# Attention in front of two feed-forward layers: scores as two 64-row products, the softmax reciprocal on GpSimd, evacuations re-dealt

## The chip, the core and the metric

One core of one Trainium2 chip runs the whole program. The metric is device time in microseconds of one execution; several executions of the kernel are timed and the median is compared. Engines are named as the profile names them: PE is TensorE, PEld its weight loads, DVE is VectorE, ACT is ScalarE, POOL is GpSimd, SP is SyncE, which issues nearly all the transfers of the stage that matters here.

## The reference

Windowed attention over 4 batches of 8 heads (576 positions, 64 elements a head; half of the heads see the last 32 positions, the other half every fourth of the last 128), then a gated layer, then a second layer, all in float32:

```python
    scores = scale * np.matmul(q, k.transpose(0, 1, 3, 2))
    ...
    scores = np.where(masks[None, :, :, :], scores, -1000000000.0)
    scores = scores - np.max(scores, axis=-1, keepdims=True)
    attn = np.exp(scores)
    attn = attn / (np.sum(attn, axis=-1, keepdims=True) + 1e-09)
    return np.matmul(attn, v).astype(np.float32)
...
    g = x @ w_gate
    silu = g * (1.0 / (1.0 + np.exp(-g)))
    val = x @ w_val
    return (silu * val @ w_out).astype(np.float32)
...
    h = x @ w_in
    g = h - np.tanh(h)
    return (g @ w_out).astype(np.float32)
```

The first layer is 512 to 1536 to 512, the second 512 to 2048 to 512, on 2304 tokens.

## The kernel before

**Attention.** The work is cut into 48 units. A unit is one pair of heads and three blocks of 64 queries; positions of the dilated heads are laid out so that every block needs 96 neighbouring keys. For each unit SP loads a tile `q` (L452; the queries of the two heads stand block-diagonally with zeros beside them, so that the tile's 128 rows are head 0's 64 elements and head 1's 64, and the keys behind them) and a tile `v` (L453). Then, in this order:

- `scores`, PE L419: three products of 128 rows by 128 columns, 96 keys wide, into one PSUM bank `ps`. A product in float32 leaves two records in the trace, so a unit has six.
- `maxima`, DVE L424: mask and row maximum. `exps`, ACT L430: exponentials and their row sums `sm`.
- `invert`, DVE L434 and L435: adds 1e-9 to `sm` (128 x 3) and takes the reciprocal.
- `norm`, POOL L438: multiplies the exponentials by it.
- `turn`, PE L444: three transpositions into a bank `pt`. `evac`: copies `pt` to SBUF, on DVE (L448) for every second unit and on ACT (L450) for the others.
- `mix`, PE L476, once for three units: products with `v`, 64 columns wide, the two heads in the two halves of the output; then ACT L489 and DVE L492 write them, split in two float32r parts, to the tiles `x` of the first layer.

**Layers.** Weights come by SP (L315) and are converted by ACT L318 and DVE L322, L326, L331, L300, L303. Each layer is made of products that PE runs in blocks: L508 (first tiles of layer 1, going up, six records a block), L519 (the seven-product scheme, going up and down), L775 and L795 (going down).

**Order.** A planner (`Plan.order`) simulates tasks with costs and priorities written as constants, and each engine's instructions are then emitted in the order of its start times. On the chip every engine runs its own list in that order and waits where a semaphore makes it. `Plan.fill` puts products on a constant tile (`idle`, L398) into PE's list where the planner saw PE idle. The constants that the change touches: `LEAD` and `SLACK` (how early a weight is loaded, how much later than its modelled landing it may be used), `DELAY_7` (how long a down product stands back), `SECOND` (spacing of the first group's weights), `FIRST_FAR` (assumed latency between engines).

Of the kernel before, what the change touches and what calls it, by code (L numbers as in the profile page):

```python
# [11 lines left out]
F32 = mybir.dt.float32  # L12
# [8 lines left out]
WINDOW, DIL = 32, 4  # L21
# [68 lines left out]
class Task:  # L90
    def __init__(self, n, eng, dur, prio, emit, deps, bufs, gives, lat, port, work):
        self.lat, self.n, self.eng, self.dur, self.prio, self.emit = lat, n, eng, dur, prio, emit
        self.port, self.work = port, work
        self.deps, self.bufs, self.gives = [d for d in deps if d is not None], list(bufs), gives
        self.fresh = None
        self.then, self.ready, self.start, self.left = [], 0.0, None, len(self.deps)


class Plan:
    ENGINES = ("PE", "DVE", "ACT", "POOL", "DMA", "NONE")  # L100

    def __init__(self, rings):
        self.tasks, self.free = [], {r: list(range(n)) for r, n in rings.items()}

    def add(self, eng, dur, prio, emit, deps=(), bufs=(), gives=None, lat=None, port=False, work=0.0):
# [6 lines left out]
    def rates(self, queues):  # L112
        heads = [e for e in queues if queues[e]]
        return [queues[e] for e in heads], [DMA_SHARE[e] for e in heads] if len(heads) > 1 else [1.0]

    def order(self):
        for t in self.tasks:
# [7 lines left out]
        while True:  # L125
            moved = True
            while moved:
                moved = False
                for e in self.ENGINES:
                    if busy[e] > now:  # L130
                        continue
                    best = None
                    for t in waiting[e]:
                        if t.ready > now + 1e-9 or (best is not None and (t.prio, t.n) >= (best.prio, best.n)):
                            continue
                        if t.port and port[0] != e and port[1] > now + 1e-9:
                            continue
                        need = {}
                        for b in t.bufs:
                            if b.slot is None:  # L140
                                need[b.ring] = need.get(b.ring, 0) + 1
                        if all(len(self.free[r]) >= n for r, n in need.items()):
# [7 lines left out]
                    best.start, busy[e] = now, now + best.dur  # L150
                    if best.port:
# [56 lines left out]


NEAR, FAR = 0.2, 0.7  # L210
FIRST_FAR, ATT_FAR = 0.3, 0.5
ISSUE, LAUNCH, LAND = 0.45, 1.1, 0.7
DMA_SHARE = {"DMA": 0.4, "POOL": 0.6}

ATT0, ATT_STEP = -30.0, 0.3
CONV0 = -24.0
LEAD = 28
DELAY = 7
ON_DVE = {(2, 1)}
SEEDED = {(1, 2), (1, 3)}  # L220
DELAY_7 = 8
MM = 0.174
V_LATE, MASK_LATE, PLAIN_FIRST = 10, 4.0, True
TOGETHER, FEW, SOON = 3, 2, 0
PASSING = 0
SECOND = 2.0
IDLE, SPARE, IDLE_UNTIL = 0.214, 0.5, 60.0
Y_SOON, DELAY_7D = 30.0, 11.0
APART = {(1, 0, 0), (1, 0, 1)}
SLACK = 2.0  # L230
SUM_DMA = 3.9
Q_DMA, V_DMA, W_DMA = 1.12, 0.5, 1.65
QUICK = 0.5
HURRY = 20.0
WARM = 10
# [8 lines left out]
def attention_then_two_ffns(ctx, tc, qk, vt, masks, w1, w2, out):  # L244
# [33 lines left out]
    new_q = ring("q", [P, UN * P + UT + WINDOW], F32)  # L278
# [7 lines left out]
    make_identity(nc, ident)  # L286
    alpha = const.tile([P, 1], F32, name="alpha")
    nc.gpsimd.memset(alpha, ALPHA)
    nthr = const.tile([P, 1], F32, name="nthr")
    nc.gpsimd.memset(nthr, -THR * THR)  # L290
    warm = const.tile([P, 512], mybir.dt.bfloat16, name="warm")
# [117 lines left out]
    def attention(b, hp, g, prio, evac_on):  # L409

        q, v, e, nm, sm, at = new_q(), new_v(), new_e(), new_nm(), new_sm(), new_at()
        ps, pt = new_ps(), new_ps()
        kinds = MASK_OF[hp // (NP // 2)][UN * g:UN * g + UN]
# [38 lines left out]
        a = add_att("DMA", ISSUE, prio, lambda: nc.sync.dma_start(out=q(), in_=qk[b, hp, g]), bufs=[q], lat=NEAR, work=Q_DMA)  # L452
        got_v = add_att("DMA", ISSUE, prio + V_LATE, lambda: nc.sync.dma_start(out=v(), in_=vt[b, hp, g]), bufs=[v], lat=NEAR, work=V_DMA)  # L453
# [7 lines left out]
        a.fresh = idle(pt)  # L461
        a = add_att(evac_on, 0.48 if evac_on == "DVE" else 0.38, prio, evac, [a], [pt, at])
        return (b, hp, g), v, at, [a, got_v]

# [78 lines left out]
            res.append((ps, a))  # L543
        return res

    def seven_up(c1, c2, sums, parts, prio):
# [18 lines left out]
        def sum22():  # L565
            nc.vector.tensor_tensor(out=e(), in0=pe()[:, :TT], in1=e(), op=ALU.add)

        p1 = pe_task(pa, (wa, 0), B11, True, [], [pb, pe])
        p5 = pe_task(pe, (w31, 1), T1, True, [], [pa, pb])
        soon = prio - HURRY  # L570
        sb = plan.add("ACT", 0.39, soon, lambda: seed(pb, pa), [p1], [pa, pb], lat=QUICK)
        ke = plan.add("ACT", 0.39, soon, keep, [p5], [pe, e], lat=QUICK)
        c11 = pe_task(pa, (wa, 1), B21, False, [sb])
        p6 = pe_task(pb, (w24, 0), T2, False, [sb])
        sc = plan.add("ACT", 0.39, soon, lambda: seed(pe, pb), [p6, ke], [pb, pe], lat=QUICK)
# [19 lines left out]
    def times_gate(g, a, prio, whole):  # L595
        s = new_t()

        def tanh():
            nc.scalar.activation(out=s(), in_=g()[:, :TT], func=AF.Tanh, scale=0.5)
# [5 lines left out]
            nc.scalar.activation(out=s(), in_=g()[:, :TT], func=AF.Silu)  # L605

        if whole:
            return s, plan.add("ACT", 0.39, prio, silu, [a], [g, s])
# [345 lines left out]
    def finish(layer, h, prio, raw=False):  # L954
        if layer == 1:
            (g, a), v = h
            whole = state["k"] >= 2
            return times_val(times_gate(g, a, prio, whole), v, prio, 1.0 if whole else 0.5, raw)
        (h, a), = h
        return cubic(h, a, prio)  # L960

# [6 lines left out]
    for layer, sizes in ((1, GROUPS1), (2, GROUPS2)):  # L968
        k = 0
        for turn, n in enumerate(sizes):  # L970
# [25 lines left out]
            for p in order:  # L996
# [3 lines left out]
                more = {"early": early} if layer == 2 and last else {}  # L1000
                if p in sevens:
                    blocks = parts_of(p, before == (layer, p), when - 12.0, begun)
                    q = [seven_up(ws[0][c], ws[1][c], extra[c], blocks, when + 0.01 * c) for c in ups]
# [191 lines left out]
```

## Time and profile before

| | before |
|---|---|
| median of 3 timed executions | 880.81 us (879.83 to 880.93) |
| the profiled execution, its own time | 881.28 us |
| its span, first to last instruction | 879.5 us |
| granted TensorE clock, mean | 0.998 |

The span is what the trace shows; 1.8 us of the profiled execution's time lie around it. Times in a trace count from the span's start. A record of PE is one matrix instruction; their ends are modelled, so starts tell more than ends.

### The profile page before, as it was taken

How to read it: one execution, taken by the hardware profiler on the slowest of the kernel's cores; microseconds unless marked ns; L12 is line 12 of the kernel's file. 1: busy time of each engine (PE TensorE's matmuls, PEld its weight loads, DVE VectorE, ACT ScalarE, POOL GpSimd, SP SyncE). 2: the span in 40 equal slices, each digit the busy share in tenths (PEclk: the TensorE clock that was granted, in tenths of full speed). 3: DMA queues.
4: the chain of work that ended last, by engine and by line, in shares of the span. 5: the costliest groups of instructions: out<-in, count | busy, mean ns of one | idle time of the engine just before them, and what ended most of it. 6: DMA issues, size and time to landing. Idle time of an engine off the chain costs nothing.

```text
span 879.5 us, 15336 instructions
## 1 busy us (share of the span) xinstructions
PE 864.4 (98%) x5240; PEld 814.5 (93%) x5242; DVE 729.1 (83%) x1738; ACT 584.2 (66%) x1516; POOL 88.3 (10%) x116
## 2 busy tenths in 40 slices
PE   8999999999999999999999999999999999999996
PEld 5789999999999999999999999889989989898995
DVE  6999999988788788788759999898787777765675
ACT  6889857768668668568658787666666656564540
POOL 2333300000000000000000000001101010111100
PEclk9999999999999999999999999999999999999999
DMA  9999353675785785777895558899979796968995
GB/s 276 282 281 266 111 205 131 228 247 173 195 258 122 208 246 122 208 225 195 252 322 215 207 199 320 255 202 270 218 220 225 177 253 165 229 131 207 248 295 213
DMA packets 48951, 193.53 MB, mean 220 GB/s; under 512 B 5600, under 2 KB 10720, under 8 KB 48864
## 3 DMA queue, kind: packets, MB, share of 16 engines
q1 hardware_dynamic: 40224, 145.28, 48.0%
q0 software_dynamic: 8640, 47.19, 29.1%
q8 instruction: 43, 0.70, 0.3%
q14 instruction: 44, 0.36, 0.1%
HBM read 119.31 MB, written 73.14 MB: 219 GB/s over the span
## 4 chain that ended last, share of the span: by engine, by line
PE 91%; DVE 4%; DMA 3%; ACT 1%; issue 0%; POOL 0%; SPq 0%; ACTq 0%; POOLq 0%
PE ps L519 53%; PE ps L795 23%; PE ps L775 7%; PE ps L508 3%; PE ps L419 2%; DMA q<-qk 2%; PE ps L476 2%; DMA st<-w 1%; PE ps L444 1%; DVE e L424 1%; PE ps L914 1%; DVE x L492 0%; ACT e L430 0%; DVE u L331 0%; DVE u L326 0%
## 5 line engine op out<-in xcount | busy, mean ns | idle before, releaser
L519 PE MATMUL ps<-x,wc 128*128 128x384 f32 x2316 | 427.2, 336 | 0.0
L519 PEld LDWEIGHTS ps<-x,wc 128*128 128x128 f32 x2316 | 407.3, 188 | 4.6
L795 PE MATMUL ps<-wc,y 128*128 128x512 f32 (+1 forms) x870 | 208.7, 391 | 0.0
L795 PEld LDWEIGHTS ps<-wc,y 128*128 128x128 f32 x870 | 161.9, 188 | 32.2 <-ACT acc L688 0.4
L688 ACT ACTIVATE acc<-ps 128x512 f32<-128x512 f32 (+1 forms) x134 | 74.7, 560 | 71.9 <-PE ps L795 56.8
L715 POOL DMA_DIRECT2D sum<-acc x60 | 52.6, 876 | 673.9 <-ACT acc L688 259.7
L590 DVE TENSOR_TENSOR y<-t,y 128x384 fp32r<-128x384 f32 x168 | 92.2, 553 | 26.4 <-ACT y L587 26.2
L587 ACT ACTIVATE y<-t 128x384 fp32r<-128x384 f32 x168 | 86.4, 518 | 23.7 <-DVE t L655 9.5
L530 ACT ACTIVATE ps<-ps 128x384 f32<-128x384 f32 x156 | 73.7, 476 | 24.1 <-PE ps L519 20.1
L300 ACT ACTIVATE wc<-u 128x512 fp32r<-128x512 f32 x108 | 67.3, 631 | 27.1 <-PE ps L519 19.9
L303 DVE TENSOR_TENSOR wc<-u,wc 128x512 fp32r<-128x512 f32 x108 | 74.3, 697 | 5.7 <-ACT wc L300 4.1
L563 DVE TENSOR_TENSOR ps<-ps,t 128x384 f32<-128x384 f32 x56 | 31.5, 562 | 41.0 <-PE ps L519 40.9
L775 PE MATMUL ps<-y,wc 128*128 128x384 f32 x336 | 62.9, 337 | 0.0
L652 DVE SCALAR_TENSOR_TENSOR t<-t 128x384 f32<-128x384 f32 x96 | 52.7, 550 | 8.8 <-ACT t L649 8.2
L775 PEld LDWEIGHTS ps<-y,wc 128*128 128x128 f32 x336 | 58.8, 188 | 0.1
L430 ACT ACTIVATE e<-e,nm 128x96 f32<-128x96 f32 x144 | 52.0, 368 | 8.0 <-DVE nm L424 8.0
L649 ACT ACTIVATE t<-ps 128x384 f32<-128x384 f32 x72 | 35.0, 486 | 28.9 <-DVE ps L563 17.8
L318 ACT ACTIVATE u<-st 128x512 f32<-128x512 f32 x68 | 44.9, 666 | 12.6 <-DMA st<-w 9.5
L326 DVE SCALAR_TENSOR_TENSOR u<-st,u 128x512 uint32<-128x512 uint32 x68 | 46.8, 691 | 0.6
L331 DVE SCALAR_TENSOR_TENSOR u<-st,u 128x512 uint32<-128x512 uint32 x68 | 46.7, 689 | 0.4
L519 PE MATMUL ps<-y,wc 128*128 128x384 f32 x198 | 45.3, 337 | 0.0
L419 PE MATMUL ps<-q 128*128 128x96 f32 x288 | 39.7, 278 | 5.2 <-DMA q<-qk 2.5
(87 smaller groups left out, 1095.2 us busy)
## 6 DMA issues: line engine op xcount, KB each, us to landing
x<-part SPq DMA_DIRECT2D x66, 768.0 KB, 7.1
sum<-acc POOLq DMA_DIRECT2D x60, 768.0 KB, 9.3
st<-w SPq DMA_DIRECT2D x68, 512.0 KB, 6.7
q<-qk SPq DMA_DIRECT2D x48, 304.0 KB, 7.3
sum<-acc SPq DMA_DIRECT2D x12, 768.0 KB, 5.6
part<-x SPq DMA_DIRECT2D x12, 768.0 KB, 3.9
acc<-sum SPq DMA_DIRECT2D x12, 768.0 KB, 7.3
v<-vt SPq DMA_DIRECT2D x48, 144.0 KB, 7.2
```

Of the source, the lines that this page charges most:

```text
L300: nc.scalar.activation(out=w()[:, 0, :], in_=u(), func=AF.Copy)
L303: nc.vector.tensor_tensor(out=w()[:, 1, :], in0=u(), in1=w()[:, 0, :].bitcast(F32), op=ALU.subtract)
L419: nc.tensor.matmul(ps()[:, i * KT:(i + 1) * KT], lhsT=q()[:, i * P:(i + 1) * P], rhs=q()[:, k0:k0 + KT], start=True, stop=True)
L519: nc.tensor.matmul(ps()[:, :TT], lhsT=w()[:, i, c:c + P], rhs=rhs, start=(start and n == 0), stop=(n == 3 * len(cols) - 1), skip_group_che ...
L530: nc.scalar.activation(out=ps()[:, :TT], in_=src()[:, :TT], func=AF.Copy)
L587: nc.scalar.activation(out=y()[:, 0, :], in_=s(), func=AF.Copy)
L590: nc.vector.tensor_tensor(out=y()[:, 1, :], in0=s(), in1=y()[:, 0, :].bitcast(F32), op=ALU.subtract)
L652: nc.vector.scalar_tensor_tensor(out=sq(), in0=sq(), scalar=E0 / E1, in1=sq(), op0=ALU.add, op1=ALU.mult)
L688: nc.scalar.activation(out=o, in_=ps()[:, :c1 - c0], func=AF.Copy)
L715: nc.gpsimd.dma_start(out=keep, in_=at(), accum_op=ALU.add)
L775: nc.tensor.matmul(ps()[:, :TT], lhsT=w[2][0]()[:, a, m * P:(m + 1) * P], rhs=y[0]()[:, bb, :], start=(start and n == 0), stop=(n == 3 * l ...
L795: nc.tensor.matmul(ps()[:, :c1 - c0], lhsT=y[0]()[:, a, s * P:(s + 1) * P], rhs=w[1][0]()[:, bb, c0:c1], start=(n == 0), stop=(n == 3 * le ...
```

## The change

Three edits in `attention`, and new constants and rules in the planner, which put every engine's list in another order.

- The product of two heads becomes two products, rows 0 to 63 into output partitions 0 to 63 and rows 64 to 127 into 64 to 127, each with 64 columns and 96 keys. The zeros of `q` are no longer read; the transfer that brings the tile is the same (`Q_PARTS = 1`).
- `invert` goes to POOL: an addition and a `pow` with exponent -1 (a constant tile `minus`), both 128 x 3.
- Evacuations are dealt DVE, DVE, ACT in turn.

```diff
-FIRST_FAR, ATT_FAR = 0.3, 0.5
+FIRST_FAR, ATT_FAR = 0.4, 0.5
...
-LEAD = 28
+LEAD = 25
...
-DELAY_7 = 8
+DELAY_7 = 6
 MM = 0.174
+SCORES = 0.56
+INVERT, INV_POOL = 'POOL', 0.5
+EVAC = ('DVE', 'DVE', 'ACT')
+LEAVE, KEEP_T = (5, 6), 1
...
-SECOND = 2.0
+SECOND = 1
...
-SLACK = 2.0
+SLACK = 1.5
...
+Q_PARTS, V_POOL, ISSUE_POOL = 1, False, 0.62
...
+                        if t.takes and (len(self.free["t"]) < (KEEP_T if t.takes == "t" else 0) or any(b.slot is None for c in self.older(t.case) for b in c[t.takes])
+                                        or t.takes == "ps" and any(b.slot is None for b in t.case["x"])):
+                            continue
+                        if t.leave and sum(b.slot is not None and b.users > 0 for b in self.fronts) >= t.leave:
+                            continue
...
             for i in range(UN):
-                k0 = UN * P + QT * i
-                nc.tensor.matmul(ps()[:, i * KT:(i + 1) * KT], lhsT=q()[:, i * P:(i + 1) * P],
-                                 rhs=q()[:, k0:k0 + KT], start=True, stop=True)
+                k0 = (UT if Q_PARTS == 3 else UN * P) + QT * i
+                for h2 in range(2):
+                    of, c = slice(D * h2, D * h2 + D), QT * i if Q_PARTS == 3 else P * i + QT * h2
+                    nc.tensor.matmul(ps()[of, i * KT:(i + 1) * KT], lhsT=q()[of, c:c + QT],
+                                     rhs=q()[of, k0:k0 + KT], start=True, stop=True)
...
         def invert():
-            nc.vector.tensor_scalar_add(sm(), sm(), 1e-9)
-            nc.vector.reciprocal(out=sm(), in_=sm())
+            if INVERT == "DVE":
+                nc.vector.tensor_scalar_add(sm(), sm(), 1e-9)
+                nc.vector.reciprocal(out=sm(), in_=sm())
+            else:
+                nc.gpsimd.tensor_scalar_add(sm(), sm(), 1e-9)
+                nc.gpsimd.tensor_tensor(out=sm(), in0=sm(), in1=minus, op=ALU.pow)
...
-        a = add_att("PE", 0.67, prio, scores, [a], [ps, q])
-        a.fresh = idle(ps)
+        a = add_att("PE", SCORES, prio, scores, got_q, [ps, q])
+        a.fresh, a.leave = idle(ps), LEAVE[0]
...
-        a = add_att("DVE", 0.31, prio, invert, [a], [sm])
+        a = add_att(INVERT, 0.31 if INVERT == "DVE" else INV_POOL, prio, invert, [a], [sm], port=INVERT == "POOL")
...
-        fronts.append(attention(*unit, ATT0 + ATT_STEP * n, ("DVE", "ACT")[n % 2]))
+        fronts.append(attention(*unit, ATT0 + ATT_STEP * n, EVAC[n % len(EVAC)]))
```

`LEAVE` lets the planner start a unit's scores only while fewer than five of the stage's banks are taken, and its transposition while fewer than six are. `KEEP_T` and `takes` hold the products and copies of a seven-product block that feeds another one back until the blocks begun before it have their buffers.

PE's list, from the 26th unit's scores to the block behind the 32nd's, before (`q` marks scores, `ident` a transposition, `at,v` a mix, `x,wc` a block of layer 1):

```order
L419 MATMUL ps_1009<-q_810 128x96 x3
L508 MATMUL ps_1026<-x_346,wc_884 128x384 x6
L444 MATMUL ps_1044<-ident,e_912 96x128 x3
...
L419 MATMUL ps_1095<-q_861 128x96 x3
L419 MATMUL ps_1111<-q_879 128x96 x3
L444 MATMUL ps_1125<-ident,e_940 96x128 x3
L508 MATMUL ps_1026<-x_448,wc_884 128x384 x6
...
L419 MATMUL ps_1224<-q_1006 128x96 x3
L444 MATMUL ps_1237<-ident,e_1090 96x128 x3
L419 MATMUL ps_1244<-q_1024 128x96 x3
L508 MATMUL ps_1257<-x_694,wc_356 128x384 x6
```

and with the change, over the same units:

```order
L440 MATMUL ps_1091<-q_843 64x96 x6
L547 MATMUL ps_1112<-x_380,wc_961 128x384 x6
L547 MATMUL ps_1131<-x_766,wc_375 128x384 x6
...
L440 MATMUL ps_1198<-q_928 64x96 x6
L547 MATMUL ps_1112<-x_483,wc_961 128x384 x6
L440 MATMUL ps_1237<-q_950 64x96 x6
L440 MATMUL ps_1249<-q_988 64x96 x6
L469 MATMUL ps_1262<-ident,e_1140 96x128 x3
L547 MATMUL ps_1131<-x_485,wc_375 128x384 x6
...
L440 MATMUL ps_1359<-q_1100 64x96 x6
L440 MATMUL ps_1370<-q_1110 64x96 x6
L547 MATMUL ps_1386<-x_766,wc_782 128x384 x6
```

Two more blocks of layer 1 stand between these scores: ahead of the 32nd unit's scores PE's list has ten of them instead of eight, with 26 transpositions and 8 mixes as before, and four more filler products.

SP's list up to the 32nd `q`, before:

```order
L452 DMA q_861<-qk 128x608
L315 DMA st_868<-w 128x512
L452 DMA q_879<-qk 128x608
L452 DMA q_910<-qk 128x608
L452 DMA q_927<-qk 128x608
L453 DMA v_979<-vt 96x384
L453 DMA v_990<-vt 96x384
L453 DMA v_997<-vt 96x384
L452 DMA q_1006<-qk 128x608
L452 DMA q_1024<-qk 128x608
```

and with the change:

```order
L487 DMA q_928<-qk 128x608
L333 DMA st_933<-w 128x512
L487 DMA q_950<-qk 128x608
L492 DMA v_965<-vt 96x384
L487 DMA q_988<-qk 128x608
L492 DMA v_1051<-vt 96x384
L492 DMA v_1062<-vt 96x384
L487 DMA q_1069<-qk 128x608
L492 DMA v_1083<-vt 96x384
L487 DMA q_1100<-qk 128x608
L487 DMA q_1110<-qk 128x608
```

Only the places of the `v` transfers move here: at the 32nd `q` both lists have issued 32 `q`, 26 `v`, 6 weights and the masks.

POOL's list gains two instructions for each unit, here of the third and fourth unit with the change:

```order
L459 TENSOR_SCALAR sm_187<-sm_187 128x3
L460 TENSOR_TENSOR sm_187<-sm_187,minus 128x3
L463 TENSOR_TENSOR e_143<-e_143,sm_170 128x288
L463 TENSOR_TENSOR e_165<-e_165,sm_187 128x288
L459 TENSOR_SCALAR sm_212<-sm_212 128x3
```

Before, POOL's list held the third kind alone; a unit's multiplication may now stand behind the next unit's reciprocal.

## Rows read from the trace of the kernel before

**Rows 1.** The page: span, and busy time, share and instructions of each engine.

```profile
span 879.5 us, 15336 instructions
PE 864.4 (98%) x5240; PEld 814.5 (93%) x5242; DVE 729.1 (83%) x1738; ACT 584.2 (66%) x1516; POOL 88.3 (10%) x116
```

**Rows 2.** Five stretches: length, busy per engine (records), PE clock, DMA share, GB/s.

```profile
0.00:20.00 20.00, 17.11 (x126) 11.82 (x128) 12.08 (x73) 12.48 (x52) 4.76 (x14) 1.00 0.91 277
20.00:66.30 46.30, 42.04 (x495) 37.58 (x495) 44.76 (x256) 40.70 (x200) 15.81 (x22) 1.00 1.04 282
66.30:112.60 46.30, 46.29 (x553) 43.55 (x553) 44.42 (x230) 39.44 (x188) 15.16 (x21) 1.00 0.63 176
112.60:860.00 747.40, 746.60 (x4011) 711.22 (x4010) 618.74 (x1166) 489.91 (x1076) 52.59 (x60) 1.00 0.77 218
860.00:879.50 19.50, 12.36 (x62) 10.36 (x60) 9.13 (x18) 1.63 (x4) 0.00 (x0) 0.91 0.55 202
```

**Rows 3.** The chain that ended last, 57 to 100: start, length, what.

```profile
57.30 8.87 DMA q<-qk
...
66.31 0.88 PE ps L419 x6
...
68.26 0.33 PE ps L444 x3
68.58 1.05 PE ps L508 x6
...
70.29 0.64 PE ps L419 x6
70.93 1.20 PE ps L476 x36
72.13 0.46 PE ps L444 x3
...
97.57 1.20 PE ps L476 x36
98.77 1.25 PE ps L508 x6
```

**Rows 4.** DMA issues, 0 to 110: count, KB each, median us to landing.

```profile
q<-qk SPq DMA_DIRECT2D x48, 304.0 KB, 7.3
v<-vt SPq DMA_DIRECT2D x48, 144.0 KB, 7.2
```

**Rows 5.** PE's waits in 20 to 66.3: in total, times, longest.

```profile
PE ps L419 <- DMA q<-qk: 1.1, 2, 0.7
PE ps L419 <- DVE nm L424: 1.1, 3, 0.5
```

**Rows 6.** Blocks L508 alone, by stretch: PE busy (records), PEld busy (records).

```profile
20.00:66.30 46.30, 10.38 (x48) 8.00 (x48) 1.00 1.04 282
66.30:112.60 46.30, 17.19 (x84) 14.19 (x84) 1.00 0.63 176
```

**Rows 7.** Groups by line, 0 to 110: count, busy, mean ns, idle before.

```profile
L438 POOL TENSOR_TENSOR e<-e,sm 128x288 f32<-128x288 f32 x48 | 35.0, 731 | 71.6 <-DVE sm L435 22.8 <-ACT e L430 16.0 <-PE ps L444 10.1
...
L448 DVE COPY at<-ps 96x384 f32<-96x384 f32 x23 | 12.5, 544 | 1.3 <-PE ps L444 1.3
...
L450 ACT ACTIVATE at<-ps 96x384 f32<-96x384 f32 x24 | 12.0, 498 | 5.0 <-PE ps L444 4.8
L434 DVE TENSOR_SCALAR sm<-sm 128x3 f32<-128x3 f32 x48 | 11.4, 237 | 0.9 <-ACT e L430 0.9
...
L435 DVE RECIPROCAL sm<-sm 128x3 f32<-128x3 f32 x48 | 8.4, 176 | 1.7
...
L288 POOL MEMSET alpha<- 128x1 f32 x1 | 0.1, 99 | 0.0
```

**Rows 8.** Waits after 100 that touch weights or PE: in total, times, longest.

```profile
ACT u L318 <- DMA st<-w: 9.5, 6, 3.5
...
PE ps L519 <- ACT ps L530: 0.8, 1, 0.8
```

More of the change, by code (lines that the diff above doesn't have):

```diff
@@ L94, in __init__ @@
         self.deps, self.bufs, self.gives = [d for d in deps if d is not None], list(bufs), gives
-        self.fresh = None
+        self.fresh, self.leave, self.case, self.takes = None, 0, None, False
         self.then, self.ready, self.start, self.left = [], 0.0, None, len(self.deps)
@@ L102, in __init__ @@
     def __init__(self, rings):
+        self.begun, self.fronts = [], []
         self.tasks, self.free = [], {r: list(range(n)) for r, n in rings.items()}
@@ L114, in rates, with older @@
         return [queues[e] for e in heads], [DMA_SHARE[e] for e in heads] if len(heads) > 1 else [1.0]
+    def older(self, case):
+        return self.begun[:next((i for i, c in enumerate(self.begun) if c is case), None)]
     def order(self):
@@ L141, in order @@
                                 need[b.ring] = need.get(b.ring, 0) + 1
-                        if all(len(self.free[r]) >= n for r, n in need.items()):
+                        if all(len(self.free[r]) >= n  for r, n in need.items()):
                             best = t
@@ L150, in order @@
                     best.start, busy[e] = now, now + best.dur
+                    if best.case is not None and not any(c is best.case for c in self.begun):
+                        self.begun.append(best.case)
                     if best.port:
@@ L288, in attention_then_two_ffns @@
     nc.gpsimd.memset(alpha, ALPHA)
+    minus = const.tile([P, UN], F32, name="minus")
+    nc.gpsimd.memset(minus, -1.0)
     nthr = const.tile([P, 1], F32, name="nthr")
@@ L412, in attention @@
         ps, pt = new_ps(), new_ps()
+        plan.fronts += [ps, pt]
         kinds = MASK_OF[hp // (NP // 2)][UN * g:UN * g + UN]
@@ L450, in evac @@
                 nc.scalar.activation(out=at(), in_=pt()[:KT, :UN * P], func=AF.Copy)
-        a = add_att("DMA", ISSUE, prio, lambda: nc.sync.dma_start(out=q(), in_=qk[b, hp, g]), bufs=[q], lat=NEAR, work=Q_DMA)
-        got_v = add_att("DMA", ISSUE, prio + V_LATE, lambda: nc.sync.dma_start(out=v(), in_=vt[b, hp, g]), bufs=[v], lat=NEAR, work=V_DMA)
-        a = add_att("PE", 0.67, prio, scores, [a], [ps, q])
-        a.fresh = idle(ps)
+        src = qk[b, hp, g]
+        if Q_PARTS == 1:
+            moves = [(q, lambda: q(), src, 1.0)]
+        elif Q_PARTS == 2:
+            moves = [(q, lambda: q()[:D, :], src[:D, :], 0.5), (q, lambda: q()[D:, QT:], src[D:, QT:], 0.45)]
+        else:
+            moves = [(q, lambda h2=h2: q()[D * h2:D * h2 + D, :UT].rearrange("p (i c) -> p i c", c=QT),
+                      src[D * h2:D * h2 + D, :UN * P].rearrange("p (i c) -> p i c", c=P)[:, :, QT * h2:QT * h2 + QT], 0.23)
+                     for h2 in range(2)]
+            moves.append((q, lambda: q()[:, UT:], src[:, UN * P:], 0.4))
+        got_q = [add_att("DMA", ISSUE, prio, lambda o=o, i=i: nc.sync.dma_start(out=o(), in_=i), bufs=[q], lat=NEAR, work=Q_DMA * w)
+                 for _, o, i, w in moves]
+        if V_POOL:
+            got_v = add_att("POOL", ISSUE_POOL, prio + V_LATE, lambda: nc.gpsimd.dma_start(out=v(), in_=vt[b, hp, g]), bufs=[v], lat=NEAR, work=V_DMA)
+        else:
+            got_v = add_att("DMA", ISSUE, prio + V_LATE, lambda: nc.sync.dma_start(out=v(), in_=vt[b, hp, g]), bufs=[v], lat=NEAR, work=V_DMA)
+        a = add_att("PE", SCORES, prio, scores, got_q, [ps, q])
+        a.fresh, a.leave = idle(ps), LEAVE[0]
         a = add_att("DVE", 0.54, prio, maxima, [a] + got_mask[:1 + (max(kinds) > 1)], [ps, e, nm])
         a = add_att("ACT", 1.09, prio, exps, [a], [e, nm, sm])
-        a = add_att("DVE", 0.31, prio, invert, [a], [sm])
+        a = add_att(INVERT, 0.31 if INVERT == "DVE" else INV_POOL, prio, invert, [a], [sm], port=INVERT == "POOL")
         a = add_att("POOL", 0.63, prio, norm, [a], [e, sm], port=True)
         a = add_att("PE", 0.31, prio, turn, [a], [e, pt])
-        a.fresh = idle(pt)
+        a.fresh, a.leave = idle(pt), LEAVE[1]
         a = add_att(evac_on, 0.48 if evac_on == "DVE" else 0.38, prio, evac, [a], [pt, at])
@@ L544, in plain_up, with seven_up @@
         return res
-    def seven_up(c1, c2, sums, parts, prio):
+    cases = [{"ps": [], "t": [], "x": []}]
+    def seven_up(c1, c2, sums, parts, prio, raw):
         (wa, da, _), (wb, db, _), ((w24, d24), (w31, d31)) = c1, c2, sums
@@ L566, in sum22 @@
             nc.vector.tensor_tensor(out=e(), in0=pe()[:, :TT], in1=e(), op=ALU.add)
+        cases[-1]["t"].append(e)
+        cases[-1]["ps"] += [pa, pb, pe]
+        cases[-1]["x"] += [b for b, _ in parts]
         p1 = pe_task(pa, (wa, 0), B11, True, [], [pb, pe])
         p5 = pe_task(pe, (w31, 1), T1, True, [], [pa, pb])
+        for a in (p1, p5):
+            a.case, a.takes = cases[-1], raw and "ps"
         soon = prio - HURRY
@@ L572, in seven_up @@
         ke = plan.add("ACT", 0.39, soon, keep, [p5], [pe, e], lat=QUICK)
+        ke.case, ke.takes = cases[-1], raw and "t"
         c11 = pe_task(pa, (wa, 1), B21, False, [sb])
@@ L593, in split_y, with times_gate @@
         return y, plan.add("DVE", 0.47, prio, low, [a], [s, y], port=True)
-    def times_gate(g, a, prio, whole):
+    def times_gate(g, a, prio, whole, raw):
         s = new_t()
+        cases[-1]["t"].append(s)
         def tanh():
@@ L607, in times_gate @@
         if whole:
-            return s, plan.add("ACT", 0.39, prio, silu, [a], [g, s])
+            a = plan.add("ACT", 0.39, prio, silu, [a], [g, s])
+            a.case, a.takes = cases[-1], raw and "t"
+            return s, a
         a = plan.add("ACT", 0.39, prio, tanh, [a], [g, s])
@@ L1002, in attention_then_two_ffns @@
                     blocks = parts_of(p, before == (layer, p), when - 12.0, begun)
-                    q = [seven_up(ws[0][c], ws[1][c], extra[c], blocks, when + 0.01 * c) for c in ups]
+                    cases.append({"ps": [], "t": [], "x": []})
+                    q = [seven_up(ws[0][c], ws[1][c], extra[c], blocks, when + 0.01 * c, p in down7) for c in ups]
                     res = {(i, t): [q[c][2 * i + j] for c in ups] for i in range(2) for j, t in enumerate(tiles)}
```

4 lines of the change are left out of this document (2 added, 2 removed).

## The prediction

> **What bounds the kernel now.** I read the page's first part first: PE is busy 864.4 us of a span of 879.5, so all idle time of PE together is 15.1 us [rows 1]. Then the same by stretches, cut where PE's idle time ends [rows 2]. PE idles 20.00 - 17.11 = 2.9 us in the first 20, 46.30 - 42.04 = 4.26 us from 20 to 66.3, nothing (0.01) from 66.3 to 112.6, 0.8 in the long middle and 7.1 in the tail, where the last results are written. The clock is granted in full (1.00, the 2.4 GHz level) but for the tail. So the change can give something in only two ways: by filling the 4.26 us, or by making the work that PE has from 66.3 on smaller. In the stretch 20 to 66.3 two others are as good as full: DVE with 44.76 us of 46.30, and the transfers, with a share of 1.04; POOL has 15.81. The chain says which of the two ends it: a transfer of `q` that takes 8.87 us from 57.30, and at once behind its landing the scores of the 32nd unit at 66.31 [rows 3]. Of a `q` it is typical to take 7.3 us from issue to landing, and of a `v` 7.2 though it is half as large [rows 4]: they queue. In PE's own waits of that stretch transfers of `q` and DVE's maxima are level, 1.1 us each [rows 5].
>
> The reading that I build on: the 32nd scores come when the queue of transfers has come to them; behind them PE is never without work, and the end of the kernel lies as far behind 66.3 as PE has work left in its list. What PE has done before that moment is gained, and what is added behind it is paid in full.
>
> **A, the blocks that move ahead of the 32nd scores.** Ahead of them the trace has 48 records of L508 [rows 6], eight blocks of six. In the changed list there are ten, with as many transpositions and mixes. One block takes 1.05 us on the chain [rows 3], so 2 x 1.05 = 2.1 us less is left behind. The transfers ahead of the 32nd `q` are the same in number and kind, so I keep its moment at 66.3. Is there room ahead of it? Two blocks take 2.1 us; the 22 scores in the stretch take 1.3 more (worked out under B); 3.4 together, of 4.26 idle. It fits if nearly all waiting goes. Bounds: -2.1 if it fits, 0 if PE waits for those blocks' inputs or comes to the 32nd scores that much later.
>
> **B, the scores as two products of 64 rows.** Before, six records take 0.64 us on the chain, 0.107 each; a transposition, whose width is the other way round (96 columns of weights, 128 streamed), takes 0.33 / 3 = 0.11 [rows 3]. So a record goes by the larger of the two widths, 128 in both. The new ones have 64 and 96, which makes 0.11 x 96 / 128 = 0.082. The nearest row for two halves side by side is the mix, L476: 36 records 64 wide in 1.20 us [rows 3]. One by one they would be 36 x 0.055 = 1.98; side by side 18 x 0.055 = 0.98. So the halves do run side by side, with 0.22 over. A unit of scores then is 6 x 0.082 = 0.49 us instead of 0.64, 0.15 less. But the mix shows a second thing: the transposition right behind it takes 0.46 instead of 0.33, and the block right behind another one 1.25 instead of 1.05 [rows 3]. Leaving the halved array costs 0.13 at least, and part of the 0.22 is entering it. I charge a group of scores 0.13 for leaving and half of the 0.22 for entering, 0.24 together, since the 0.22 also holds the pairs' own issue. Behind the 32nd (itself included as the first) 17 units stand in the new list in 13 groups, some of two units; I count 16 that are paid in full: 16 x -0.15 = -2.4 and 13 x 0.24 = +3.1, so +0.7 us. Bounds: -2.4 with no cost of changing over, +2.1 with 0.35 a group. Ahead of the 32nd, 22 units in 19 groups: -3.3 + 4.6 = +1.3, paid out of idle time.
>
> In the mix both halves read the same rows; in the new scores each half has rows of its own and writes into the same bank. No row of this trace shows such a pair. The Trainium skill's page TensorEngine Tiling (Array Packing), section Restrictions and Gotchas, says that different row tiles cannot access the same PSUM bank at the same time. By that rule the pairs would run one after the other; it is the third rival below, with its own price.
>
> **C, the reciprocal and the evacuations.** DVE loses 48 x (0.237 + 0.176) = 19.8 us and gets eight evacuations more, 8 x 0.544 = 4.4; ACT loses 8 x 0.498 = 4.0 [rows 7]. For the 22 units of 20 to 66.3 that is 7.1 us off DVE's 44.76, so DVE would be busy 81% there and no longer full. On PE's path behind 66.3 it is worth nothing, as PE idles 0.01 there [rows 2]; ahead of it, it is what lets A fit, and is not counted twice. POOL gets two instructions of three elements a lane. Their cost is not in the trace: at least the 0.099 of a MEMSET each, at most the 0.731 of the multiplication of 288 [rows 7], so 0.2 to 1.46 a unit. Over 22 units that makes POOL 15.81 + 4.4 = 20.2 to 15.81 + 32 = 48 us of 46.30. I take 0.5 a unit (27 us), nearer to the small end, for three elements; only the far end would make POOL the bound, by under 2 us. A hand-over from DVE to POOL goes away: POOL waited 22.8 us for L435 [rows 7], which cost PE nothing directly. Queued behind the two new instructions on POOL is only the next multiplication, and behind that its transposition.
>
> **D, the rest of the plan.** Weights are planned with 0.5 us less margin. ACT waited six times for a weight, 9.5 us together, and one of these waits reached PE, 0.8 us [rows 8]. Bounds: -0.8 if that one goes, +3.0 if six waits grow by 0.5 and all reach PE. I take 0: PE's work of the long middle is the same, and the waits of ACT were hidden five times in six.
>
> **Sum.** The profiled execution is 881.28 us, 1.8 more than its span; -2.1 + 0.7 + 0 + 0 gives 879.9. The median of the timed runs is 0.47 below the profiled one, so 880.81 - 1.4 = 879.4 us. One thing to say once: differences under 0.2%, 1.8 us, can hardly be told from none here; the forecast lies just inside.
>
> **The rivals.**
> 1. *Changing over is cheap.* If the scores pay nothing for entering and leaving, B is -2.4, the two blocks fit easily, and the wait of 0.8 us goes: -2.1 - 2.4 - 0.8 = -5.3, 875.5 us. For it: the 32nd scores begin right as their transfer lands, and a change-over can hide in such a wait. Against it: every mix in the chain shows it [rows 3].
> 2. *PE's waiting from 20 to 66.3 stays, because it is waiting for transfers.* Then the 3.4 us of added work there push the 32nd scores back by up to 3.4: -1.4 + 3.4 = +2.0, 882.8 us, slower. It decides when more than 3.2 of the 4.26 us stay. For it: the DMA share of 1.04, which the change leaves alone [rows 2]. Against it: half of the waits named are DVE's [rows 5], and DVE gets 7 us.
> 3. *The halves don't run side by side* (the same bank). A unit is 12 x 0.082 = 0.98, +0.34 over before. Behind the 32nd: 16 x 0.34 + 3.1 = 8.5; ahead: 22 x 0.34 + 4.6 + 2.1 = 14.2 against 4.26 idle, 9.9 late; less 2.1: +16.3, 897 us.
> 4. *Nothing comes of it:* the two blocks wait for tiles `x` or weights that are not earlier, the scores cost what they cost; 880.8.
>
> POOL becomes a bound only above 2.1 us a unit (46.30 / 22); each 0.1 beyond would cost 4.8 us over 48 units. I give that 0.03, inside the third.
>
> **How the numbers follow.** Forecast 0.45, with 877.8 to 880.8 as its own range (two fifths of it beyond the 1.8 us); rival 1 0.22; rival 2 0.13; rival 3 with POOL 0.06; rival 4 0.14. Faster: 0.18 + 0.22 + a little = 0.42. Slower: most of rivals 2 and 3 = 0.17. The same: 0.41. The range goes from rival 1 to rival 2, 875.6 to 882.8, and leaves out the third and the tails.
>
> **What would show it.** A: the 32nd scores at 66 to 67 us with ten blocks ahead of them, and PE's idle time from 20 to there near 1 us. B: the records of a pair of halves starting within some ns of each other, a lone unit of scores at 0.5 us, and 0.4 to 0.46 for the transposition behind it; a start every 0.08 us would be rival 3. C: DVE at some 80% from 20 to 66, POOL under 30 us. D: PE idle near 0.8 us between 112 and 860. The forecast is wrong if the 32nd scores move by more than a microsecond either way, or if PE's long middle gets waits that it did not have.

## The result and the profile after

| | before | after |
|---|---|---|
| median of the timed executions (4 each) | 880.87 us (879.83 to 881.07) | 891.31 us (889.92 to 892.27) |
| ratio, 95% interval | | 1.012 (1.0102 to 1.0137) |
| the profiled execution, and its span | 881.28 us, 879.5 us | 890.56 us, 888.7 us |

The change makes the kernel 10.4 us slower: more than the forecast of 879.4, and more than its upper end of 882.8. Below, a ratio and its interval are an estimate of their own and can differ from the quotient of the two medians by up to 0.0009. One of the ten executions of e1b_constant took 1420.24 us at a granted clock of 0.557 and is left out of its ratio. The page's first part, of the changed kernel, to be held against [rows 1]:

```profile
span 888.7 us, 15934 instructions
PE 867.8 (98%) x5534; PEld 806.8 (91%) x5534; DVE 716.9 (81%) x1650; ACT 583.6 (66%) x1508; POOL 148.3 (17%) x213
```

PE's idle time is 888.7 - 867.8 = 20.9 us instead of 15.1, so 5.8 of the span's 9.2 us are waiting and 3.4 are more busy time. DVE lost 12 us of work and nothing came of it; POOL gained 60. The five stretches of [rows 2], after:

```profile
0.00:20.00 20.00, 14.09 (x120) 7.88 (x120) 7.23 (x50) 9.99 (x43) 11.66 (x27) 0.94 0.92 269
20.00:66.30 46.30, 43.61 (x636) 35.45 (x635) 43.68 (x220) 39.11 (x187) 40.27 (x59) 0.99 1.04 275
66.30:112.60 46.30, 42.46 (x615) 35.50 (x613) 37.46 (x190) 38.98 (x194) 41.53 (x65) 1.00 0.67 209
112.60:860.00 747.40, 746.05 (x4065) 709.49 (x4065) 611.39 (x1161) 490.22 (x1074) 54.87 (x64) 1.00 0.75 213
860.00:879.50 19.50, 19.50 (x93) 16.76 (x93) 15.58 (x31) 5.30 (x15) 0.00 (x0) 1.00 0.77 269
```

In 20 to 66.3 PE idles 2.7 us, less than the 4.26 of before: the forecast gain is half there. It is lost on both sides of it. In the first 20 us PE idles 5.9 instead of 2.9, and from 66.3 to 112.6, where it had never waited, 3.84. In all three the column that has changed most is POOL's: 11.66, 40.27 and 41.53 instead of 4.76, 15.81 and 15.16. (The last row holds more PE work only because the program ends later.) PE's waits over the whole span, longest sums first, name it:

```profile
PE ps L469 <- POOL e L463: 6.2, 5, 1.8
PE ps L469 <- DMA st<-w: 2.0, 1, 2.0
PE ps L515 <- issue: 1.3, 1, 1.3
PE ps L558 <- ACT ps L569: 1.1, 1, 1.1
```

Line 469 is the transposition, line 463 POOL's multiplication. The same wait stood in none of the rows on which the prediction rests; over 0 to 120 it had been 0.6 us in two waits before. POOL's groups, 0 to 120 (line 459 is the addition, 460 the power), and the spread of two of them (shortest, median and longest in ns):

```profile
L460 POOL TENSOR_TENSOR sm<-sm,minus 128x3 f32<-128x3 f32 x48 | 45.9, 956 | 4.0
L463 POOL TENSOR_TENSOR e<-e,sm 128x288 f32<-128x288 f32 x48 | 33.4, 709 | 1.6
L459 POOL TENSOR_SCALAR sm<-sm 128x3 f32<-128x3 f32 x48 | 16.0, 333 | 13.1 <-ACT e L451 9.5
```

```profile
L459 POOL TENSOR_SCALAR sm<-sm x48: 232/233/1689, 7.2 to 112.4; 128x3 f32<-128x3 f32 x48
L460 POOL TENSOR_TENSOR sm<-sm,minus x48: 878/879/2223, 7.5 to 112.8; 128x3 f32<-128x3 f32 x48
```

The power of three elements a lane takes longer than the multiplication of 288. With the addition, the two new instructions cost 0.956 + 0.333 = 1.29 us a unit where I took 0.5. Most records are as short as the medians and some are drawn out: in this trace all 13 additions of over 0.26 us and 10 of the 11 powers of over 0.90 us overlap a weight conversion on DVE (L321 to L370), of the others 3 of 35 and 7 of 37. No run tests whether that is the cause. The chain that ended last, cut at 135 us, shows what that does (start, length, what):

```profile
7.21 0.24 POOL sm L459
7.52 0.90 POOL sm L460
8.49 0.67 POOL e L463
9.24 0.24 POOL sm L459
...
15.40 1.16 POOL sm L460
16.63 0.68 POOL e L463
17.35 0.53 PE ps L469 x3
17.88 1.15 PE ps L440 x12
...
22.56 0.64 PE ps L440 x12
...
28.32 0.46 PE ps L469 x3
...
69.56 1.14 PE ps L440 x24
70.69 1.24 PE ps L547 x6
...
100.92 0.24 POOL sm L459
101.24 1.29 POOL sm L460
...
114.29 0.68 POOL e L463
115.01 0.53 PE ps L469 x3
```

From one unit's addition to the next one's are 9.24 - 7.21 = 2.03 us, with the gaps between instructions. Over all 48 units it is more: POOL's three groups are busy 45.9 + 33.4 + 16.0 = 95.3 us, and of the 4.0 + 1.6 + 13.1 = 18.7 us of idle time before them 9.5 are waits for ACT, so that 9.2 are gaps of its own. Together they make 104.5 us, 2.18 a unit. Of the waits for ACT the first, 5.9 us, ends with the first row sums; from then on POOL waits 3.6 us in all and is otherwise taken up to the last multiplication. POOL alone carries the chain from 7.2 to 17.3 and again from 100.9 to 115.0; in both stretches PE waits for the transpositions that are next in its list. The row at 69.56 holds the 31st and 32nd units' scores, so the 32nd comes near 70 instead of 66.3. The last transposition comes at 115.0; before, it started at 108.8, the third of the three units in `108.34 0.98 PE ps L444 x9` of that chain. The 200th record of the layers' products, by which the order around the attention no longer matters, starts at 129.5 instead of 122.2: 7.3 of the 9.2 us have been lost by then.

The early waiting is followed by a second cost. PE's clock by stretches of a few us (length, then busy us of PE, PEld, DVE, ACT and POOL, PE clock, DMA share, GB/s):

```profile
10.00:12.00 2.00, 0.70 (x11) 0.29 (x7) 1.39 (x13) 1.52 (x8) 1.83 (x4) 1.00 1.01 406
...
14.00:16.00 2.00, 1.16 (x7) 0.56 (x6) 0.38 (x1) 2.00 (x9) 1.75 (x4) 1.00 1.05 261
16.00:17.00 1.00, 0.23 (x2) 0.00 (x0) 0.51 (x2) 0.28 (x1) 0.92 (x2) 1.00 1.11 257
...
18.00:21.00 3.00, 3.00 (x26) 2.11 (x26) 2.28 (x10) 1.44 (x7) 1.41 (x3) 0.50 1.07 266
```

After the idle stretches the granted clock falls to 0.50, the 1.2 GHz level, for 18 to 21 us; a unit of scores there takes 1.15 us instead of the 0.64 at 22.56 (chain). Three microseconds at half speed are 1.5 us of work, nearly half of the 3.4 us that PE is busier. Idle time of that size does not always bring it: e3 and e12 below idle 6.1 and 6.0 us in the first 20 and keep 1.00 from 18 to 21.

### The profile page after: what moved, and what is told of

It is laid out like the page before. It is cut to its first block, busy times and chain, and to the rows that moved or that the text cites. A ratio compares the mean times of both kernels' runs of the same rounds, so it can differ in the third digit from the quotient of the medians.

```text
span 888.7 us, 15934 instructions
## 1 busy us (share of the span) xinstructions
PE 867.8 (98%) x5534; PEld 806.8 (91%) x5534; DVE 716.9 (81%) x1650; ACT 583.6 (66%) x1508; POOL 148.3 (17%) x213
## 4 chain that ended last, share of the span: by engine, by line
PE 88%; DVE 5%; POOL 3%; DMA 2%; issue 1%; ACT 1%; POOLq 0%; SPq 0%; DVEq 0%; ACTq 0%
PE ps L558 52%; PE ps L845 20%; PE ps L825 6%; PE ps L547 3%; PE ps L440 2%; PE ps L515 2%; PE ps L469 2%; DMA st<-w 2%; POOL sm L460 1%; DVE x L909 1%; POOL e L463 1%; DVE acc L924 1%; DVE t L705 0%; DVE y L637 0%; DVE t L702 0%
## 5 line engine op out<-in xcount | busy, mean ns | idle before, releaser
L558 PE MATMUL ps<-x,wc 128*128 128x384 f32 x2316 | 426.0, 336 | 1.1 <-ACT ps L569 1.1
L558 PEld LDWEIGHTS ps<-x,wc 128*128 128x128 f32 x2316 | 407.4, 188 | 5.8 <-ACT ps L569 1.5
L321 DVE TENSOR_TENSOR wc<-u,wc 128x512 fp32r<-128x512 f32 x108 | 74.0, 693 | 5.4 <-ACT wc L318 4.0
L460 POOL TENSOR_TENSOR sm<-sm,minus 128x3 f32<-128x3 f32 x48 | 45.9, 956 | 4.0
L558 PE MATMUL ps<-y,wc 128*128 128x384 f32 x198 | 45.3, 337 | 0.0
```

Of the source, the lines that this page charges most:

```text
L321: nc.vector.tensor_tensor(out=w()[:, 1, :], in0=u(), in1=w()[:, 0, :].bitcast(F32), op=ALU.subtract)
L460: nc.gpsimd.tensor_tensor(out=sm(), in0=sm(), in1=minus, op=ALU.pow)
L558: nc.tensor.matmul(ps()[:, :TT], lhsT=w()[:, i, c:c + P], rhs=rhs, start=(start and n == 0), stop=(n == 3 * len(cols) - 1), skip_group_che ...
```

## The experiments

**Theory 1:** POOL. The power makes a unit cost about as much on POOL as the whole stage gives it, and PE's transpositions wait. **Theory 2:** the order and the halves of scores are what costs, and POOL's waits only show it. (Where an expectation names a theory 3, theory 2 is the halves alone and theory 3 the order.) The first runs take the power away, and each part alone.

**e1_no_pow**: the changed order, a short product in the power's place.

```diff
-                nc.gpsimd.tensor_tensor(out=sm(), in0=sm(), in1=minus, op=ALU.pow)
+                nc.gpsimd.tensor_tensor(out=sm(), in0=sm(), in1=minus, op=ALU.mult)
```

> The changed kernel with its own order of instructions, only the power replaced by a multiplication of the same tile on the same engine (so the softmax is not normalised rightly; everything else is computed). Theory 1, POOL: the power takes 0.96 us a unit on average in the trace and the addition 0.33, against 0.5 planned for both; with a short instruction in its place POOL is no longer late, and the time falls from 891.3 to 880 to 883. Theory 2, scores: the changes of PE between whole and halved array cost the time; it stays at 890 to 892. Theory 3, order: the new order of instructions itself costs it; it stays at 889 to 892.

The whole took 3196.48 us, since the large unnormalised values send the program into a long branch behind the last layer; that time says nothing here. Ahead of it the trace is readable. PE's waits up to 120, first rows:

```profile
PE ps L440 <- DMA q<-qk: 4.5, 9, 0.9
...
PE ps L469 <- POOL e L463: 0.3, 2, 0.2
```

The product takes 257 ns where the power takes 956, and PE's waiting for POOL falls from 6.2 us to 0.3. What is left is mostly the waiting for `q`.

**e1b_constant**: the same with values that stay small, so that its time can be read: each row is scaled by a constant 0.04.

```diff
-    nc.gpsimd.memset(minus, -1.0)
+    nc.gpsimd.memset(minus, 0.2)
-                nc.gpsimd.tensor_tensor(out=sm(), in0=sm(), in1=minus, op=ALU.pow)
+                nc.gpsimd.tensor_tensor(out=sm(), in0=minus, in1=minus, op=ALU.mult)
```

> The changed kernel with its own order; the power is replaced by a short product of the constant tile with itself (0.04), so the rows are scaled by a constant instead of normalised, and the values stay in the range in which the last layer's short form runs. The first such run took the long branch at the end and its time says nothing, but its trace up to there had the 32nd scores at 66.4 us and the stage's end 1.3 us earlier than the kernel before. If the length of the power is what costs the time: 880 to 882.5, with 1 to 2 us lost again in the second layer. If something else does: above 886.

880.96 us (median of 10) beside 881.52 of the kernel before, ratio 0.9999 (0.9989 to 1.0009). With order, halves and evacuations all as in the change, the 10.4 us are gone. The two stretches of e1b:

```profile
20.00:66.30 46.30, 45.01 (x656) 37.47 (x658) 44.58 (x227) 40.94 (x201) 30.66 (x66) 1.00 1.05 285
66.30:112.60 46.30, 46.30 (x643) 40.14 (x643) 41.11 (x194) 38.22 (x182) 22.21 (x58) 1.00 0.78 218
```

PE idles 1.3 us from 20 to 66.3 and nothing in the stretch behind. (The traced execution, 878.85 us, is the fastest of the ten.) Theory 1 holds for the whole of the loss; theory 2 has at most 0.1% left.

**e4_before_pow**: the other way round, the kernel before with nothing changed but the addition and the power on POOL.

```diff
-            nc.vector.tensor_scalar_add(sm(), sm(), 1e-9)
-            nc.vector.reciprocal(out=sm(), in_=sm())
+            nc.gpsimd.tensor_scalar_add(sm(), sm(), 1e-9)
+            nc.gpsimd.tensor_tensor(out=sm(), in0=sm(), in1=minus, op=ALU.pow)
```

> The kernel before with its own order, only the addition and the reciprocal (as a power) moved to POOL, at the places where they stood on DVE. Theory 1: POOL needs 0.7 + 1.2 us a unit, 48 units are 91 us, as long as the whole stage; 887 to 893. Theory 2 and 3: DVE is relieved by 19.8 us and nothing else changes; 879 to 881.5.

897.57 us (896.57 to 898.43), ratio 1.0177 (1.0158 to 1.0196). PE's waits up to 120, first row:

```profile
PE ps L446 <- POOL e L440: 14.6, 15, 2.8
```

The addition and the power on POOL do it without the rest of the change, and worse in an order that wasn't laid out for them: the time lies above the range of theory 1, which had counted 1.2 us for the two and no gaps.

**e3_full_scores**: the changed kernel with scores as three products of 128 rows again.

```diff
-                for h2 in range(2):
-                    of, c = slice(D * h2, D * h2 + D), ...
-                    nc.tensor.matmul(ps()[of, i * KT:(i + 1) * KT], lhsT=q()[of, c:c + QT],
-                                     rhs=q()[of, k0:k0 + KT], start=True, stop=True)
+                nc.tensor.matmul(ps()[:, i * KT:(i + 1) * KT], lhsT=q()[:, i * P:(i + 1) * P],
+                                 rhs=q()[:, k0:k0 + KT], start=True, stop=True)
```

> The changed kernel with its own order, only the scores as three products of 128 rows again. Theory 1: PE waits for POOL whatever the scores take, so the time moves by 1.5 us at most, 889.8 to 892.8. Theory 2: 35 changes into and out of the halved array go away, 0.285 us each (what a mix shows), against 48 x 0.15 given up: 3 us or more less, 881 to 888. Theory 3: no change, 890 to 892.

890.47 us (889.38 to 891.04), ratio 1.0098 (1.0081 to 1.0116) beside the changed kernel's 1.012: the halves are not what costs the 10 us. **e9_constant_full_scores** makes the same edit in e1b, where POOL hides nothing:

> The run with the constant in place of the power (rows scaled by 0.04 and not normalised), its order kept, and the scores as three products of 128 rows again. Term B said that 48 units cost 48 x -0.15 + 35 x 0.24 = 1.2 us more as halves, of which 0.7 show in the end; so 0 to 2 us less than the run with the constant (881.0), 879 to 881. If changing over is cheap, as in rival 1: 3 to 5 us more, 884 to 886.

879.59 us beside 880.64, ratio 0.9984 (0.9972 to 0.9995). Against e1b's 0.9999 the halves cost about 0.0015 x 881 = 1.3 us; the two intervals meet, and the quotients of the medians (0.9994 and 0.9988) lie closer, so that this alone doesn't prove it.

**e10_no_add**: the power stays on POOL, the addition of 1e-9 is left out. How close to its limit is POOL?

```diff
-                nc.gpsimd.tensor_scalar_add(sm(), sm(), 1e-9)
```

> The changed kernel with its own order, without the addition of 1e-9 on POOL (1 + 1e-9 is 1 in float32). POOL's work a unit falls from 2.0 to 1.66 us. If POOL's length is what PE waits for: 48 x 0.33 = 16 us less of POOL work in a stage where it is 87 to 90% busy, so more than half of the loss goes, 883 to 887. If not: 889.5 to 892.

881.46 us (880.50 to 884.01), ratio 1.0004 (0.9989 to 1.0019). POOL's groups and the two stretches of e10:

```profile
L459 POOL TENSOR_TENSOR sm<-sm,minus 128x3 f32<-128x3 f32 x48 | 47.1, 986 | 22.5 <-ACT e L451 19.9 <-PE ps L440 1.3 <-PE ps L468 1.1
L462 POOL TENSOR_TENSOR e<-e,sm 128x288 f32<-128x288 f32 x48 | 33.1, 700 | 1.6
```

```profile
20.00:66.30 46.30, 43.62 (x646) 35.97 (x643) 44.26 (x222) 40.08 (x197) 35.81 (x43) 1.00 1.02 281
66.30:112.60 46.30, 46.30 (x660) 39.84 (x660) 41.81 (x197) 39.15 (x192) 33.21 (x42) 1.00 0.73 211
```

The power costs as much as ever, and a third of a microsecond a unit gives back nearly the whole loss; I had looked for 883 to 887. Counted as above, POOL now needs 80.2 us of work and 24.1 - 22.3 = 1.8 us of gaps, 82.0 in all or 1.71 a unit, and the rest of its time it waits for others. The last transposition starts at 107.3 instead of 115.0. It is not the longer way of a single unit that counts: the power alone is still 0.986 - 0.413 = 0.57 us longer than the two instructions on DVE were, and costs nothing that shows here. So somewhere between 1.71 and 2.18 us a unit POOL turns from an engine that waits into one that is waited for.

**e12_pow_width**: e1b with a power of the first column alone behind the short product; one execution, of 3206.98 us, since its values take the long branch again.

```diff
+                nc.gpsimd.tensor_tensor(out=sm()[:, :1], in0=sm()[:, :1], in1=minus[:, :1], op=ALU.pow)
```

> The run with the constant in place of the power, and behind it a power of the first of the three columns alone (the rows are scaled by constants and not normalised). For the trace only: if the power costs by element, (0.88 - 0.26) / 3 = 0.21 us each on top of some 0.25, it takes 0.4 to 0.5 us; if by instruction, 0.8 to 0.9.

POOL's groups of e12 (line 461 is the power, 460 the short product):

```profile
L464 POOL TENSOR_TENSOR e<-e,sm 128x288 f32<-128x288 f32 x48 | 35.7, 756 | 1.6
L461 POOL TENSOR_TENSOR sm<-sm,minus 128x1 f32<-128x1 f32 x48 | 29.3, 611 | 3.8
L459 POOL TENSOR_SCALAR sm<-sm 128x3 f32<-128x3 f32 x48 | 15.9, 331 | 12.6 <-ACT e L451 8.9
L460 POOL TENSOR_TENSOR sm<-minus 128x3 f32<-128x3 f32 x48 | 11.8, 247 | 4.0
```

One column takes 611 ns, three 956, between the two forecasts: (956 - 611) / 2 = 0.17 us for each further column, and 0.44 that do not depend on the width, if the cost is a straight line between these two. The trace says a second thing. With a shorter power but one instruction more, POOL needs 92.7 + 13.1 = 105.8 us, 2.20 a unit, as long as in the changed kernel; PE waits for it 13 times, 11.5 us in all, and the last transposition is as late, at 115.6. So it is the length of POOL's work that counts, not the power as such.

**e7_replan_cost**: the planner is told 1.2 us for the two instructions, and makes a new order.

```diff
-INVERT, INV_POOL = 'POOL', 0.5
+INVERT, INV_POOL = 'POOL', 1.2
```

> The changed kernel, the planner told 1.2 us for POOL's two instructions instead of 0.5, everything else as changed. If POOL's capacity is the limit (1.2 + 0.7 us a unit, 48 units, 91 us): 886 to 893, as PE's other work can't be moved ahead far enough. If the wrong place in the list is the limit (PE's list puts transpositions before POOL has done): below 884.

901.31 us (900.82 to 901.97), ratio 1.0233 (1.0216 to 1.0250). PE idles 4.6 us from 20 to 66.3, 4.9 from there to 112.6, and 6.3 in the long middle, where it had idled 0.8. That is above both ranges. Knowing the price, this planner doesn't lower it: its order is 10 us worse than the one that doesn't know. PE hardly waits for POOL there, 0.2 us up to 120; it waits for DVE's L531 (5.1 us) and for `q` (3.9) instead.

**The reciprocal back on DVE.** e2_inv_dve_same_plan emits it there without touching the order (`if True:` in `invert`), e6_replan_dve tells the planner (`INVERT = 'DVE'`), e13_dve_no_add leaves out the addition besides (0.2 us planned).

> The changed kernel with its own order, but the addition and a reciprocal emitted on DVE at the place where POOL's two instructions stood. Theory 1: DVE has room for 19.8 us more (37.5 to 43.7 of 46.3 busy in the two stretches), POOL keeps one instruction of 0.7 us a unit; 880 to 883. Theory 2 and 3: 889 to 892.

> The changed kernel with the reciprocal on DVE and planned there, 0.31 us; everything else as changed, the order is made anew. If the move of the reciprocal to POOL is the whole loss: 879.5 to 883. If the rest of the change (scores, evacuations, constants) costs as well: 884 to 889.

> The changed kernel with one reciprocal on DVE, without the addition, planned at 0.2 us; order made anew. The run with addition and reciprocal on DVE was at 886.0, with 7.4 us of idle PE from 20 to 112.6. If that was DVE's load: 878 to 882. If it is the place of the transfers in the new order: 884 to 888.

888.16 us, ratio 1.0069 (1.0052 to 1.0085); 886.01, 1.0056 (1.0038 to 1.0073); 884.34, 1.0036 (1.0022 to 1.0051). Theory 1 alone had 883 at most for them, and all three are above it: e2 lies between its two ranges, e6 and e13 in the upper ones, which stood for costs in the rest of the change and for the transfers' place in the new order. e1b shows no such cost in the changed order itself. From 20 to 66.3 DVE is as full as ever in the first two, and PE's waits of e6 up to 120 are of two kinds:

```profile
PE ps L440 <- DMA q<-qk: 4.2, 4, 1.2
PE ps L469 <- POOL e L463: 3.2, 5, 1.1
```

In e13 DVE has air (41.28 us of 46.30), and PE idles 3.6 there all the same, and 3.7 in the long middle; the traced execution, 887.79 us, is the slowest of its ten.

**What relief of DVE is worth by itself.** e8_before_no_add is the kernel before without the addition of 1e-9, in its own order; e15_before_no_add_replan lets the planner know (0.2 instead of 0.31).

```diff
-            nc.vector.tensor_scalar_add(sm(), sm(), 1e-9)
```

> The kernel before with its own order, without the addition of 1e-9 to the row sums (the largest exponential of a row is 1, and 1 + 1e-9 is 1 in float32). DVE loses 48 x 0.237 = 11.4 us of a stage where it is full. If DVE's load is what makes PE idle from 20 to 66 us: 877 to 879.5. If the transfers are: 880 to 881.5.

> The kernel before without the addition of 1e-9, planned anew with 0.2 us for the reciprocal, nothing else. With the old order the relief of DVE gave 0.1% at most, because PE then waited for transfers of q. If a new order can use the relief by putting blocks ahead: 876.5 to 879. If the transfers decide: 879.5 to 882.

e8: 880.52 us, ratio 0.9990 (0.9977 to 1.0002). Its stretch, and PE's first wait up to 120:

```profile
20.00:66.30 46.30, 40.73 (x498) 37.86 (x499) 39.69 (x229) 39.55 (x195) 15.67 (x22) 1.00 0.98 278
```

```profile
PE ps L419 <- DMA q<-qk: 5.8, 7, 1.6
```

DVE goes from 44.76 to 39.69, and PE idles 5.6 us instead of 4.26: nearly all of it, 4.8, is waiting for transfers now. e15 takes 883.70, ratio 1.0035 (1.0021 to 1.0049), above both ranges, with 10 us less work on DVE than before. It differs from e8 in the order alone, so a new order of this planner can cost 3 us by itself, for no reason that its costs show.

**e16_no_add_full_scores**: the best of the parts, as a version: the changed order with the power on POOL, no addition, and whole scores (e10's and e3's edits).

> The changed kernel with its own order, without the addition on POOL and with the scores as products of 128 rows: the two costs that the other runs found are taken away and the rest of the change stays. 881.5 (without the addition) less 1.4 (what whole scores gave behind the constant) is 880.1, level with the kernel before or 0.1 to 0.3% faster, 878.5 to 880.5. If the two don't add up: 881 or more.

880.23 us (877.34 to 881.82, 12 runs) beside 881.03 (17 runs), ratio 0.9989 (0.9976 to 1.0001): some 11 us better than the changed kernel, and level with the kernel before. e16 against e10 (1.0004) is again 0.0015 for the halves, and again the intervals meet. Its second stretch has no idle time on PE, its first 2.1 us:

```profile
20.00:66.30 46.30, 44.20 (x528) 40.54 (x523) 44.52 (x226) 41.06 (x201) 37.10 (x43) 1.00 1.03 290
66.30:112.60 46.30, 46.30 (x556) 43.90 (x555) 43.12 (x200) 39.22 (x189) 33.32 (x42) 1.00 0.76 212
```

## Why the prediction was wrong, step by step

**The step that failed is C**, in its size and in its limit. "I take 0.5 a unit (27 us), nearer to the small end, for three elements": it was 1.29, near the far end of 1.46. The reason given, that few elements make a short instruction, holds for a product (0.257) and not for a power (0.956); the rows of before held nothing that computes such a function on POOL, and the two ends of 0.2 and 1.46 should have carried equal weight. With the multiplication and POOL's own gaps a unit takes 2.18 us, where 0.5 + 0.731 = 1.23 was forecast, and so POOL is the bound: the case to which I gave 0.03.

The second half of the step is its limit: "POOL becomes a bound only above 2.1 us a unit (46.30 / 22)". It leaves out the gaps, and it was read from one stretch alone, while the loss arose in the two beside it. Over the whole chain POOL's 104.5 us begin at 7.2, when the first row sums come, so they can't end before 111.7, and with the 3.6 us of later waits for ACT they end near 115. The last transposition stood at 108.8 before, and in the changed order with less work on POOL it stands at 105.0 (e1b) or 107.3 (e10): 8 to 10 us earlier than the changed kernel's 115.0, which is the size of the loss. For the far end of my own bound, 1.46 + 0.731 = 2.19 and so close to what was measured, I wrote "by under 2 us", where my own 4.8 us for each 0.1 above 2.1 makes some 4; e1b against the changed kernel puts it at 10. (A slip beside it: rival 1's own 880.81 - 5.3 is 875.5, and the range begins at 875.6.)

**A was near right in its mechanism.** In e1b, where POOL is out of the way, the 32nd scores come in the row `64.42 1.14 PE ps L440 x24` of its chain, the second unit of which starts at 64.9, with the ten blocks ahead; forecast were 66 to 67 and about 1 us of idle time, it is 1.3. In e1, the same order with a product of the same length, they come at 66.4, so two executions differ here by 1.5 us. The gain itself isn't seen: A and B together were to give -1.4 us, a ratio of 0.9984, and e1b, without POOL's cost, is at 0.9999 (0.9989 to 1.0009). In the changed kernel itself the 32nd scores are 3.7 us late, which the prediction named as the sign that it is wrong.

**B was right in mechanism and near in size.** A pair's halves start 6 to 7 ns apart and the next pair 76 ns later, so a unit takes 6 x 82.5 = 0.495 us (forecast 0.49). With the change-over in front it takes the chain's 0.64, two units in one go 1.14, and the transposition and the block behind show the rest as they do behind a mix, 0.46 and 1.24 us. Rival 3 is refuted, and with it what I took from the Trainium skill's page TensorEngine Tiling (Array Packing), section Restrictions and Gotchas: two products that read different halves of the rows do run side by side into one PSUM bank, at least where each writes partitions of its own. In all the halves cost some 1.3 us (e9 against e1b, e16 against e10; the intervals of each pair meet, but both pairs, and e3 against the changed kernel, point the same way), where +0.7 behind the 32nd scores was forecast and +1.3 ahead of it was to be hidden.

**C's other half, the relief of DVE, came nearly in the forecast amount and bought nothing that the runs show**: over the span DVE is busy 12.2 us less (19.8 - 4.4 = 15.4 were forecast), but from 20 to 66.3 it stays at 43.68 us where I expected 81% (37.5), as 20 records of weight conversion fall into the stretch instead of 13. e8 shows that relief alone only hands the waiting over to the transfers, which was rival 2's mechanism. Why e1b, e10 and e16 stop at the time of before and don't go below is not shown: in e10's trace PE idles 13.4 us instead of 15.1, and is busy 866.2 instead of 864.4.

**D** was put at 0, with bounds of -0.8 to +3.0. Behind the 200th layer record some 2 us more are lost. The wait of 0.8 at L519 is gone, and one of 1.1 at L558 has come, behind a weight whose transfer took 10.59 us. This is the kind of wait that the bound was for, but e1b and e10 in the same order lose 0.3 to 0.6 us there; that the smaller margin causes it isn't shown. Nor is it for the wait of 2.0 us on a weight in the attention (second row of PE's waits): e3 has it too, e1b, e10 and e12 don't, and e12 is as late as the changed kernel without it.

**Open:** why the orders with the reciprocal on DVE (e2, e6, e13, e15) end 3 to 8 us above before. Full DVE may explain part of the first two and nothing of the others. Open too is what draws out some of POOL's records: at their medians the three instructions would take 0.233 + 0.879 + 0.667 = 1.78 us a unit instead of 2.00. Whole scores and a DVE reciprocal in a new order together were not tried.

## What to carry to other kernels

An operation that no row of the trace shows is priced by its kind, not by its width: bounds far apart mean that both ends are cases with chances of their own, and one run with the operation by itself settles it. The limit of an engine that serves another one in order is worked out over the whole chain that it has to carry, from its first input to its last output, with the gaps between its instructions, and not over the stretch that looked tight before: here 104.5 us from 7.2 on made the chain 8 to 10 us too long, 82.0 us cost nothing that can be told from noise, and the step between the two was one instruction of a third of a microsecond a unit.

## What was not expected of the hardware

- A power on POOL with three elements a lane takes 0.96 us in the mean (0.88 in the median, 2.22 at the longest), a product in the same place 0.26; with one element it takes 0.61.
- The products of two halves of the rows into one PSUM bank run side by side, their records 6 to 7 ns apart.
- Going from whole products to halves and back costs PE about 0.28 us a time with a transposition behind (0.64 - 0.495 in front, 0.46 - 0.33 behind) and 0.33 with a block behind (1.24 - 1.05), an estimate from the chain's rows; the forecast had 0.24.
- After 5.9 us of idle time on PE in the first 18 the changed kernel has 3 us at the 1.2 GHz level; e3 and e12, with 5.5 us in the same time, have none there.
